# Splitting the second mixer's GELU by row tiles instead of by row chunks, with a new instruction order, in a two-layer attention and mixer kernel

## The chip, the cores and the metric

The kernel runs on one core of a Trainium2 chip. The core has a matrix engine (TensorE, PE in the profile), ScalarE (ACT), VectorE (DVE), GpSimd (POOL) and SyncE (SP), which run their own instruction streams side by side and wait for one another by semaphores. The metric is device time in microseconds (us). The kernel before has a median of 1063.17 us in three runs (1063.0 to 1063.62).

## The reference, cut to what matters

Two layers, each an attention block and a mixer block, both with a residual. S = 2048 rows, D = 448, H = 16 heads of 28, F = 1792. Layer norms have neither scale nor bias.

```python
def _A_ref(x, wqkv, wo):
    qkv = (x @ wqkv).reshape(B, S, 3, H, Dh).transpose(2, 0, 3, 1, 4)
    q, k, v = qkv[0], qkv[1], qkv[2]
    p = softmax(einsum("bhqd,bhkd->bhqk", q, k) * Dh ** -0.5)
    return einsum("bhqk,bhkd->bhqd", p, v).transpose(0, 2, 1, 3).reshape(B, S, D) @ wo

def _B_ref(x, w1, w2, w3, w4):
    h = gelu(layernorm(x) @ w1)
    # the four column quarters of h are shifted by +1, -1, +2 and -2 rows
    x1 = x + shifted(h) @ w2
    return x1 + gelu(layernorm(x1) @ w3) @ w4

x = A_x
for layer in range(2):
    x = x + _A_ref(layernorm(x), A_wqkv, A_wo)
    x = x + _B_ref(layernorm(x), B_w1, B_w2, B_w3, B_w4)
```

The change is in `gelu(layernorm(x1) @ w3) @ w4`: h2 = gelu(...) has 1792 columns for each row, held transposed in SBUF as h2T, 14 chunks of 128 of those columns ("row chunks": they lie on the partitions) by the rows of x.

## The kernel before

The 2048 rows are 16 tiles of 128. Attention goes by units of query tiles: four units of 4 in the first layer; in the second three of 4 and two of 2. For each unit, group of four heads and part of the keys, TensorE makes scores (line L1441, "QK") into PSUM, ScalarE takes their exp (L1484), and TensorE multiplies the result by V (L1511, "PV"). Exps come in 775 granules, of three PSUM banks and of two (1536 and 1024 elements a partition) in turn; indices 0 to 384 are the first layer's. The scores of granule n+2 are issued as soon as the exp of granule n has emptied its banks, so two granules are in flight. A part of the exps is made on VectorE by a polynomial instead (L1396 to L1412).

All else is woven between: layer norm and transposed rows xT (L1075; transposes by DMA, by TensorE at L1037 and L1053), the projections of K and Q (L1082; copies kT at L1091 and L1094, qT at L1087 and L1089, squares for a bound on the scores at L1101 to L1105, a correction and a bias of Q at L1134 and L1344, the maximum kmax at L1118), V (L1147, L1151), the output projection (L1587), the first mixer's GELU (L1674 for a unit, L1657 for the last), and the second mixer. Most of those matmuls are cut in four 32-column pieces that run beside each other, all by the helper at L174.

The second mixer (`t_mixB`) works on parts of 2 to 4 tiles: tiles [0,1,2], [3..6], [7..10], [11,12], [13,14,15] of the first layer, and in the second the first four of these, then 13, 14 and 15 singly, whose GELU (L1802) reads PSUM. For a part, 14 groups of matmuls with w3 (third stage) fill h2T through casts by VectorE (L1805); then the GELU runs in place over h2T in two instructions (L1817); then `w4_tile` (fourth stage) multiplies each tile by w4, 14 chunks one after the other, and adds the result to the residual x_res (L1825). The two GELU instructions each take 7 row chunks of all the part's tiles. A tile of w4 takes its PSUM bank when chunks 0 to 6 are there.

ScalarE must load a table between exp and GELU (ACT_TABLE_LOAD), 24 times in all. For the parts behind the first two units the second mixer's GELU is made to stand right behind the first mixer's (GATED).

The order on every engine is fixed when the kernel is built. Generators yield operations with a planned duration, what they read and what they write; a list scheduler (`Sched`) places them by rank, the ranks coming from the latest starts of the round before. After two rounds `reorder` shifts the ranks by a table of numbers, SEEDS (L614), and a last round gives the order of each engine. So an edit of an operation or of one number can move any instruction behind it. The planner also puts filler matmuls in places where TensorE would idle. At the start GpSimd loads rows of x by DMA (L866) and clears padding (L957 to L969); `t_setup` and `t_setup2` hold that.

## Time and profile before

| | before |
|---|---|
| median of the runs | 1063.17 us (1063.0 to 1063.62) |
| the profiled execution, its own time | 1062.37 us |
| its span (first to last instruction) | 1060.3 us |
| granted TensorE clock, mean | 0.998 |
| instructions on ScalarE / TensorE matmuls | 908 / 14218 |
| first exp starts, last exp ends | 33.48, 1014.14 us |
| DMA | 41.26 MB, mean 39 GB/s |

The span is shorter than the time of its execution by 2.07 us that lie around it. Three stretches can be told apart: 33.5 us until the first exp, 980.7 us in which exps follow one another, and 46.2 us behind the last exp, with the end of the second mixer and the output. Rows of the profile name the source line, the engine, and the tiles as out<-in; an arrow in brackets names what ended the idle time before an instruction.

### The profile page before, as it was taken

The numbers are of one execution on the slowest core, as the hardware profiler recorded it, in microseconds if no ns is written. First come the engines' busy times: TensorE is split into PE (matmuls) and PEld (weight loads), VectorE is DVE, ScalarE is ACT, GpSimd is POOL, SyncE is SP. The second block draws the span as 40 slices with busy tenths as digits, with TensorE's granted clock in tenths as the row PEclk, the third lists the DMA queues.
The fourth block names the chain that finished last, engine by engine and source line by source line (L and its number), as shares of the span: only waits on it lengthen the run. The fifth ranks groups of instructions, "written<-read, shape, count | busy, mean of one in ns | idle before, by whom it ended". The sixth has DMA issues, their size and how long they took to land.

```text
span 1060.3 us, 31768 instructions
## 1 busy us (share of the span) xinstructions
PE 986.8 (93%) x14218; PEld 390.6 (37%) x14219; DVE 840.9 (79%) x1854; ACT 1003.3 (95%) x908; POOL 161.2 (15%) x177
## 2 busy tenths in 40 slices
PE   7999999999999998999998999999999999999898
PEld 5333333333333333333334333333333333443355
DVE  8999999999968775754996689999988788545463
ACT  5899999999999999999699999999999999999954
POOL 5220101210202002100332012001112020120111
PEclk9999999999999999999999999999999999999999
DMA  7222060100000000101112222010011010010000
GB/s 203 61 74 74 25 179 22 22 16 2 22 21 22 2 21 23 21 2 42 32 51 67 75 67 72 22 42 21 11 32 37 2 34 12 22 27 25 12 19 23
DMA packets 77103, 41.26 MB, mean 39 GB/s; under 512 B 61288, under 2 KB 70376, under 8 KB 76968
## 3 DMA queue, kind: packets, MB, share of 16 engines
q1 hardware_dynamic: 74856, 35.58, 12.9%
q0 software_dynamic: 2112, 3.67, 1.4%
q8 instruction: 111, 1.82, 0.7%
q14 instruction: 24, 0.20, 0.1%
HBM read 14.20 MB, written 8.13 MB: 21 GB/s over the span
## 4 chain that ended last, share of the span: by engine, by line
ACT 73%; PE 22%; DVE 4%; issue 0%; DMA 0%; POOL 0%; DVEq 0%; ACTq 0%
ACT PT L1484 66%; PE ps L174 11%; PE ps L1441 5%; PE ps L1511 3%; ACT h2T L1817 3%; PE ps L1796 1%; ACT hT L1674 1%; PE ps L1822 1%; ACT L1484 1%; DVE xn L1075 1%; ACT L1674 1%; DVE st L984 0%; DMA w<-in_A_x_dram 0%; DVE qT L1134 0%; DVE sc L935 0%
## 5 line engine op out<-in xcount | busy, mean ns | idle before, releaser
L1484 ACT ACTIVATE PT<-ps 128x1536 bf16<-128x1536 f32 (+1 forms) x775 | 879.5, 1259 | 14.4 <-PE ps L1441 13.0
L1441 PE MATMUL ps<-qT,kT 32*128 32x512 bf16 (+1 forms) x2184 | 303.0, 359 | 30.8 <-ACT PT L1484 24.9
L1511 PE MATMUL ps<-PT,vaug 128*32 128x512 bf16 (+1 forms) x2184 | 233.0, 360 | 5.1 <-ACT PT L1484 3.5
L1441 PEld LDWEIGHTS ps<-qT,kT 32*128 32x128 bf16 x2184 | 76.0, 91 | 253.9 <-ACT PT L1484 147.0
L174 PE MATMUL ps<-xT,w 128*32 128x512 bf16 (+5 forms) x2324 | 150.6, 345 | 1.0 <-DVE h2T L1805 0.4
L1805 DVE CAST h2T<-ps 128x512 bf16<-128x512 f32 (+2 forms) x126 | 73.7, 585 | 40.5 <-PE ps L174 38.2
L1511 PEld LDWEIGHTS ps<-PT,vaug 128*32 128x32 bf16 x2184 | 61.9, 94 | 108.9 <-issue 53.8
L174 PE MATMUL ps<-w,h2T 128*32 128x448 bf16 x1524 | 94.3, 354 | 6.6 <-ACT h2T L1817 3.0
L1396 DVE TENSOR_SCALAR dT<-ps 128x512 f32<-128x512 f32 x116 | 79.1, 684 | 14.8 <-PE ps L1392 11.3
L174 PE MATMUL ps<-wk_pad,zero 128*32 128x256 bf16 x1644 | 81.0, 275 | 0.0
L1407 DVE SCALAR_TENSOR_TENSOR dU<-dF 128x512 f32<-128x512 uint16 x116 | 79.3, 684 | 0.9
L1412 DVE SCALAR_TENSOR_TENSOR dT<-dU,dT 128x512 int32<-128x512 f32 x116 | 79.4, 685 | 0.8
L1409 DVE SCALAR_TENSOR_TENSOR dU<-dF,dU 128x512 f32<-128x512 uint16 x116 | 79.1, 682 | 0.7
L174 PEld LDWEIGHTS ps<-xT,w 128*32 128x32 bf16 (+1 forms) x2324 | 53.0, 95 | 53.2 <-issue 24.6
L1825 DVE SCALAR_TENSOR_TENSOR x_res<-x_res,mst,ps 128x448 f32<-128x448 f32 x32 | 21.6, 678 | 61.2 <-PE ps L174 48.2
L1105 POOL TENSOR_TENSOR sq<-qT 128x512 bf16<-128x512 bf16 (+1 forms) x32 | 31.9, 999 | 248.9 <-DVE qT L1091 191.7
L1764 POOL TENSOR_TENSOR x_res<-x_res,x1b 128x448 f32<-128x448 f32 x31 | 37.2, 1204 | 184.7 <-DVE x1b L1745 183.2
L174 PEld LDWEIGHTS ps<-w,h2T 128*32 128x32 bf16 x1524 | 38.1, 96 | 43.4 <-issue 15.3
L1105 POOL TENSOR_TENSOR sq<-kT 128x512 bf16<-128x512 bf16 (+1 forms) x32 | 31.7, 991 | 137.3 <-DVE kT L1091 90.9
L1402 DVE TENSOR_SCALAR dF<-dT 128x512 uint16<-128x512 uint16 x116 | 48.5, 418 | 0.6
L174 PEld LDWEIGHTS ps<-wk_pad,zero 128*32 128x32 bf16 x1644 | 40.0, 95 | 23.8 <-issue 19.1
L1817 ACT ACTIVATE h2T<-h2T 128x3584 bf16<-128x3584 bf16 (+2 forms) x18 | 46.9, 2605 | 0.3
(172 smaller groups left out, 1189.3 us busy)
## 6 DMA issues: line engine op xcount, KB each, us to landing
uscr<-u_sb SPq DMA_DIRECT2D x24, 256.0 KB, 2.1
uin<-uscr SPq DMA_DIRECT2D x24, 256.0 KB, 2.8
x_res<-in_A_x_dram POOLq DMA_DIRECT2D x4, 896.0 KB, 5.3
out_dram<-uin SPq DMA_DIRECT2D x16, 112.0 KB, 1.7
w<-in_B_w_dram SPq DMA_DIRECT2D x1, 1568.0 KB, 13.4
w<-in_B_w_dram SPq DMA_DIRECT2D x1, 1344.0 KB, 8.6
h2T<-in_A_wqkv_dram SPq DMA_DIRECT2D x2, 336.0 KB, 4.5
xT<-xn SPq DMA_TRANSPOSE x33, 3.7
```

The costliest lines, as they stand in the source:

```text
L174: return [self.e.matmul(out=out[c:min(c + 32, self.m)], lhsT=lhsT[:, c:min(c + 32, self.m)], rhs=rhs, start=start, stop=stop, tile_positio ...
L1105: yield op("pool", 0.1 + 0.002 * nw, lambda e, si=si: e.tensor_tensor(out=sq[:, si, 0:nw], in0=dst, in1=dst, op=ALU.mult), reads=dkeys, wr ...
L1396: yield op("dve", c_ps(cw), lambda e, b=b: e.tensor_scalar(out=dT[:, s, 0:cw], in0=ps[:, bi(b), 0:cw], scalar1=65536.0 + 127 * 128.0, scal ...
L1402: yield op("dve", c_f2b(cw), lambda e: e.tensor_scalar(out=dF[:, f, 0:cw], in0=dT[:, s, 0:cw].bitcast(U16).rearrange("p (q two) -> p q two ...
L1407: yield op("dve", c_ps(cw), lambda e: e.scalar_tensor_tensor(out=dU[:, v, 0:cw], in0=dF[:, f, 0:cw], scalar=-16384.0, in1=dF[:, f, 0:cw], ...
L1409: yield op("dve", c_ps(cw), lambda e: e.scalar_tensor_tensor(out=dU[:, v, 0:cw], in0=dF[:, f, 0:cw], scalar=EXPD * 16384.0, in1=dU[:, v, 0 ...
L1412: yield op("dve", c_ps(cw), lambda e: e.scalar_tensor_tensor(out=dT[:, s, 0:cw].bitcast(I32), in0=dU[:, v, 0:cw], scalar=EXPC * 2.0 ** -35 ...
L1441: yield op("pe", 0.012 + W / 2400.0, lambda e, bk=bk, r0=32 * j, g=g, kc=kc, q0=q0, W=W, c0=W * h: e.matmul(out=ps[:, bk, c0:c0 + W], lhsT ...
L1484: yield op("act", e_dur(n), lambda e, b0=b0, p0=p0, cnt=cnt, cw=cw: e.activation(out=PT[:, p0:p0 + cnt, 0:cw], in_=ps[:, b0:b0 + cnt, 0:cw ...
L1511: yield op("pe", 0.004 + nt * 0.0133, lambda e, j=j, rhs=rhs, vs=vs, i=i: e.matmul(out=ps[32 * j:32 * j + 32, bi(SUM), 0:128 * nt], lhsT=v ...
L1805: yield op("dve", c_ps(NW), lambda e, fch=fch, b=b: e.tensor_copy(out=h2T[:, fch, hoff:hoff + NW], in_=ps[:, bi(b), 0:NW]), reads=[("ps", ...
L1817: yield op("act", c_act(7 * NW), lambda e, f0=f0: e.activation(out=h2T[:, f0:f0 + 7, hoff:hoff + NW], in_=h2T[:, f0:f0 + 7, hoff:hoff + NW ...
```

## The change

The GELU over h2T is split by tiles: passes over two tiles (one, where an odd one is left) and all 14 row chunks. A tile of w4 takes its bank when all 14 chunks of its tile are there. The number of passes for a part stays two for 3 and 4 tiles; for 2 tiles it becomes one. In SEEDS the entries are other ones from 29639 on (95 lines of them become 122), so instructions move on all engines, throughout. Lines of the new kernel lie 27 to 28 lower.

```diff
@@ -617,95 +617,122 @@
         (3033793134, 1, 0, -44.1), 120960, 262583, (2115317989, 1, 0, -1.4), (24560949, 2, 3, 14.3), 282526, 330535, 128665, 506082,
         (2115317989, 1, 2, -6.9), 494183, 220204, 391981, 182732, 482011, 827523, 903787, 171502, 468151, 477258, 255142, 737183, 133974,
         (873278056, 1, 0, -8.0), 659964, 702438, 411030, (2992251532, 2, 0, -20.0), 356684, 480141, 383044, (2115317989, 1, 183, -0.6),
-        211184, 29639, (446382429, 5, 0, -42.4), (2115317989, 1, 2216, -1.3), 230258, 942391, 611146, 253696, 497183, (4057997978, 1, 0,
...
+        211184, 29639, (4199727191, 6, 0, -3.4), 377439, 781968, 836653, 977732, 853990, 962485, (3017015515, 1, 0, -3.9), 788647, 843800,
...
     ]
     DL = 0.58
@@ -1812,12 +1839,13 @@
                 yield ("sig", ("h2", L, tiles[0]))
                 if gated:
                     yield ("wait", ("g2", L, tiles[0]))
-                for f0 in (0, 7):
-                    hk = [(("h2T",), (fch, hoff // 128 + j)) for fch in range(f0, f0 + 7) for j in range(n)]
-                    yield op("act", c_act(7 * NW), lambda e, f0=f0: e.activation(out=h2T[:, f0:f0 + 7, hoff:hoff + NW], in_=h2T[:, f0:f0 + 7, hoff:hoff + NW], func=ACT.Gelu_apprx_tanh),
-                             reads=allk if f0 == 0 else hk, writes=hk, tab="gelu", margin=0.0 if gated or f0 else 1.0)
+                for i in range(0, n, 2):
+                    m = min(2, n - i)
+                    hk = [(("h2T",), (fch, hoff // 128 + j)) for fch in range(14) for j in range(i, i + m)]
+                    yield op("act", c_act(14 * 128 * m), lambda e, i=i, m=m: e.activation(out=h2T[:, :, hoff + 128 * i:hoff + 128 * (i + m)], in_=h2T[:, :, hoff + 128 * i:hoff + 128 * (i + m)], func=ACT.Gelu_apprx_tanh),
+                             reads=allk if i == 0 else hk, writes=hk, tab="gelu", margin=0.0 if gated or i else 1.0)
             def w4_tile(i, t):
-                b = yield ("acq", MISC, [(("h2T",), (fch, hoff // 128 + i)) for fch in range(7)])
+                b = yield ("acq", MISC, [(("h2T",), (fch, hoff // 128 + i)) for fch in range(14)])
                 for fch in range(14):
                     yield op("pe", c_mm(D), lambda e, fch=fch, i=i, b=b: e.matmul(out=ps[:, bi(b), 0:D], lhsT=h2T[:, fch, hoff + 128 * i:hoff + 128 * i + 128], rhs=w4[:, fch, :],
                                                                            start=(fch == 0), stop=(fch == 13)),
```

Three places where the order moved. First TensorE at the boundary of the layers, from the last granule of layer 0 (one L1441 matmul, L1468 in the new kernel) to layer 1's first (five of them). The rows between are the projections of layer 1's first unit (xT with wq_pad, wk_pad, wv; sq with astat sums the squares for the bound) and the fourth stage (w,h2T; 32x448 is one column piece). Before:

```order
L1441 MATMUL ps<-qT,kT 128x512
L174 MATMUL ps<-xT,wq_pad 32x512 x28
L174 MATMUL ps<-wv,xT 32x448 x16
L174 MATMUL ps<-xT,wq_pad 32x512 x32
L174 MATMUL ps<-xT,wk_pad 32x512 x16
L174 MATMUL ps<-sq,astat 32x512 x8
L174 MATMUL ps<-xT,wk_pad 32x512 x12
L174 MATMUL ps<-sq,astat 32x512 x4
L174 MATMUL ps<-xT,wk_pad 32x512 x4
L1441 MATMUL ps<-qT,kT 128x512 x5
```

Now:

```order
L1468 MATMUL ps<-qT,kT 128x512
L174 MATMUL ps<-w,h2T 32x448 x16
L174 MATMUL ps<-xT,wq_pad 32x512 x16
L174 MATMUL ps<-w,h2T 32x448 x56
L174 MATMUL ps<-xT,wk_pad 32x512 x16
L174 MATMUL ps<-xT,wq_pad 32x512 x16
L174 MATMUL ps<-sq,astat 32x512 x4
L174 MATMUL ps<-xT,wk_pad 32x512 x12
L174 MATMUL ps<-sq,astat 32x512 x4
L174 MATMUL ps<-xT,wk_pad 32x512 x4
L1468 MATMUL ps<-qT,kT 128x512 x5
```

16 and 56 pieces of the fourth stage, its last for the part [7..10], come between the two granules now, and less of Q and K; the projection of V went behind. The GELU of the part [7..10] on ScalarE stands ahead of granule 378 instead of 370.

Second the start, on GpSimd (x_res<-in_A_x_dram are the loads of rows, sc and rstd small powers, the MEMSETs padding). Before:

```order
L992 TENSOR_TENSOR rstd<-vpe,neghalf 128x2
L866 DMA x_res<-in_A_x_dram 128x4x448
L959 MEMSET vaug 128x320
L866 DMA x_res<-in_A_x_dram 128x4x448 x2
L961 MEMSET wo_pad 128x1792
L965 COPY selq<-id 32x512
L934 TENSOR_TENSOR sc<-sc,halfs 128x4
L866 DMA x_res<-in_A_x_dram 128x4x448
L967 MEMSET w 128x448
L969 MEMSET w 128x1792
```

Now:

```order
L1019 TENSOR_TENSOR rstd<-vpe,neghalf 128x2
L893 DMA x_res<-in_A_x_dram 128x4x448 x2
L986 MEMSET vaug 128x320
L893 DMA x_res<-in_A_x_dram 128x4x448 x2
L988 MEMSET wo_pad 128x1792
L961 TENSOR_TENSOR sc<-sc,halfs 128x4
L1019 TENSOR_TENSOR rstd<-vpe,neghalf 128x4
L992 COPY selq<-id 32x512
L994 MEMSET w 128x448
L996 MEMSET w 128x1792
```

The four loads stand together more closely, ahead of the clearing of wo_pad; one rstd moved ahead of selq and the last two MEMSETs. On VectorE in the same stretch, from the first copies of xT. Before:

```order
L1057 COPY xT<-ps 128x4x128 x2
L962 MEMSET zero 128x64
L963 CAST e28b<-e 128x4
L964 TENSOR_TENSOR id<-ident 32x16
L925 CAST csum<-ps 128x8
L984 BN_STATS st<-x_res 128x6
L928 COPY wsum<-ps 128x8
L1057 COPY xT<-ps 64x4x128
L930 TENSOR_SCALAR sc<-wsum 128x4
L931 RECIPROCAL sc<-sc 128x4
L932 SCALAR_TENSOR_TENSOR sc<-wsum,sc 128x4
L986 BN_AGGR mv<-st 128x2
```

Now:

```order
L1084 COPY xT<-ps 128x4x128 x3
L1084 COPY xT<-ps 64x4x128
L1011 BN_STATS st<-x_res 128x6
L989 MEMSET zero 128x64
L1013 BN_AGGR mv<-st 128x2
L1011 BN_STATS st<-x_res 128x6
L952 CAST csum<-ps 128x8
L1013 BN_AGGR mv<-st 128x2
L1128 TENSOR_TENSOR sq<-kT 128x512
L955 COPY wsum<-ps 128x8
L1011 BN_STATS st<-x_res 128x6
L1145 TENSOR_REDUCE kmaxc<-ps 128x1
```

One copy of xT more is VectorE's (ScalarE had it), and a square of K and the first kmax come ahead of the small column sums (wsum, sc), which came ahead of all K before.

Third ScalarE behind the last exp (PT are exps, uin copies for the output, hT the first mixer's GELU, h2T the second's). Before:

```order
L1484 ACTIVATE PT<-ps 128x1024 x2
L1866 ACTIVATE uin<-x_res 128x448 x3
L1657 ACT_TABLE_LOAD
L1657 ACTIVATE hT<-ps 112x128 x8
L1817 ACTIVATE h2T<-h2T 128x7x256 x2
L1042 ACTIVATE xT<-ps 128x512
L1866 ACTIVATE uin<-x_res 128x448
L1802 ACTIVATE h2T<-ps 128x128 x42
```

Now:

```order
L1511 ACTIVATE PT<-ps 128x1024 x2
L1894 ACTIVATE uin<-x_res 128x448 x2
L1069 ACTIVATE xT<-ps 128x512
L1684 ACT_TABLE_LOAD
L1684 ACTIVATE hT<-ps 112x128 x4
L1845 ACTIVATE h2T<-h2T 128x14x256
L1684 ACTIVATE hT<-ps 112x128 x4
L1069 ACTIVATE xT<-ps 128x512
L1829 ACTIVATE h2T<-ps 128x128 x42
```

One GELU pass of 14 chunks and two tiles stands between the two halves of the first mixer's GELU, where two passes of 7 chunks stood behind both; two copies for the output went to VectorE, and a copy of xT came to ScalarE.

203 rows, old and new, of the table SEEDS are left out of this document.

## The prediction

> **What bounds the kernel now.** I read the page first: the busy shares, the chain of work that ended last, and the costliest groups (line, engine, operation, count; then busy us and mean ns of one; then the idle time before them and its releaser).
>
> ```profile
> PE 986.8 (93%) x14218; PEld 390.6 (37%) x14219; DVE 840.9 (79%) x1854; ACT 1003.3 (95%) x908; POOL 161.2 (15%) x177
> ...
> ACT 73%; PE 22%; DVE 4%; issue 0%; DMA 0%; POOL 0%; DVEq 0%; ACTq 0%
> ...
> L1484 ACT ACTIVATE PT<-ps 128x1536 bf16<-128x1536 f32 (+1 forms) x775 | 879.5, 1259 | 14.4 <-PE ps L1441 13.0
> ...
> L174 PE MATMUL ps<-w,h2T 128*32 128x448 bf16 x1524 | 94.3, 354 | 6.6 <-ACT h2T L1817 3.0
> ```
>
> ScalarE is busy 95% of the span, and 879.5 us of that are the 775 exps. An exp waited only 14.4 us in all. So a microsecond counts only where ScalarE does more work, where it waits, or where it has not begun (before the first exp) or has finished (after the last). TensorE at 93% is the close second. Its 3.0 us of waits for the GELU at L1817 lie where ScalarE is itself busy with that GELU, so taking them away pays only if a later exp was waiting for the matmuls behind them.
>
> Next, ScalarE's order of time, merged (start, duration, count), and its GELU groups by shape:
>
> ```profile
> 200.04 113.19 ACT L1484 ACTIVATE PT<-ps 128x1536 bf16<-128x1536 f32 x100
> ...
> 480.16 6.41 ACT L1817 ACTIVATE h2T<-h2T 128x3584 bf16<-128x3584 bf16 x2
> 486.60 1.28 ACT L1484 ACT_TABLE_LOAD   x1
> 487.89 16.43 ACT L1484 ACTIVATE PT<-ps 128x1536 bf16<-128x1536 f32 x15
> 512.41 12.60 ACT L1484 ACTIVATE PT<-ps 128x1024 bf16<-128x1024 f32 x11 [8.10 <-PE ps L1441]
> 526.48 15.02 ACT L1484 ACTIVATE PT<-ps 128x1536 bf16<-128x1536 f32 x13 [1.46 <-PE ps L1441]
> ...
> 545.61 1.02 ACT L1484 ACTIVATE PT<-ps 128x1024 bf16<-128x1024 f32 x1 [0.79 <-PE ps L1441]
> ```
>
> ```profile
> L1817 ACT ACTIVATE h2T<-h2T 128x3584 bf16<-128x3584 bf16 x8 | 25.5, 3184 | 0.1
> L1817 ACT ACTIVATE h2T<-h2T 128x2688 bf16<-128x2688 bf16 x6 | 14.6, 2438 | 0.1
> ...
> L1817 ACT ACTIVATE h2T<-h2T 128x1792 bf16<-128x1792 bf16 x4 | 6.8, 1694 | 0.1
> ```
>
> In the middle of a layer 100 exps follow one another in 113.19 us, 1.13 us each, with no wait. The one large hole is at the layer boundary: 8.10 us before the first exp of layer 1. It is over half of all waiting.
>
> **The change part by part.** Two things are edited, the split of the GELU and the table behind the order. The sum has six terms.
>
> *1. GELU instructions.* A part of three or four tiles has two passes before and after. Four tiles are two of 3584 elements in both. Three tiles were 2 x 2438 = 4876 ns and become one of 3584 and one of 1792, 3184 + 1694 = 4878 ns. A part of two tiles was 2 x 1694 = 3388 ns and becomes one of 3184, 0.2 less. There are two such parts: **-0.4**. Table loads stay at 24 and the exps at 775. That the first two tiles' fourth-stage matmuls are whole after the first pass, and no longer stop at chunk 7, touches the 3.0 us above. I cost it at nothing: while the GELU runs, ScalarE is the engine that is late, and its next exps have scores lying ready in both bank groups. Were the cover gone, it would cost or win at most a share of those 3.0.
>
> *2. The boundary.* The rows of TensorE and VectorE there:
>
> ```profile
> 484.18 5.12 PE L174 MATMUL ps<-w,h2T 128*32 128x448 bf16 x100 [0.20 <-DVE kmaxc L1118]
> ...
> 503.06 0.38 PE L1441 MATMUL ps<-qT,kT 32*128 32x512 bf16 x1
> ...
> 511.99 0.59 PE L1441 MATMUL ps<-qT,kT 32*128 32x512 bf16 x5
> ```
>
> ```profile
> 502.97 0.68 DVE L1825 SCALAR_TENSOR_TENSOR x_res<-x_res,mst,ps 128x448 f32<-128x448 f32 x1 [3.25 <-PE ps L174]
> ...
> 509.19 0.75 DVE L1091 TENSOR_SCALAR kT<-ps,cols 128x512 bf16<-128x512 f32 x1 [0.17 <-PE ps L174]
> 509.86 1.43 DVE L1134 SCALAR_TENSOR_TENSOR qT<-ps,sc,qT 128x512 bf16<-128x512 f32 x2
> 511.20 0.64 DVE L1344 TENSOR_SCALAR qT<-qT,bcol 128x512 bf16<-128x512 bf16 x1
> ```
>
> Layer 1's first scores start at 511.99 because layer 1's Q and K need xT, which needs x_res, which needs the last fourth-stage matmuls. All of that hangs on the end of the first GELU pass, T0 = 480.16 + 3.2 = 483.36. Before, 15 exps stand behind this GELU: ScalarE runs out at 504.32 = T0 + 21.0 and starts again at 512.41 = T0 + 29.1. In the new order only 7 exps are left when the GELU ends. ScalarE then runs out at T0 + 3.2 (second pass) + 1.3 (load) + 7 exps at some 1.06 to 1.13 (7.4 to 7.9), near T0 + 11.9, 9.05 earlier. How much earlier can TensorE have the scores? The 224 narrow w4 matmuls take 51 ns each by the row of 100, and a little less where others interleave: 10.5 us. I go through the new order: the last score of layer 0 at T0 + 10.6, 16 w4 at 11.45, 16 of Q at 12.3, two residual additions of 0.68 each that release the next bank at 12.85, 56 w4 at 15.5, 16 of K at 16.35, the last tile's addition behind normalising work on VectorE at 17.1, 16 of Q at 18.0, then the chain kT 0.75, correction of Q 0.75 and bias 0.33 with their hand-offs, 20.1, and scores and the exp at T0 + 20.9. The stall is 20.9 - 11.9 = 9.0 against 8.10: **+0.9**. From below: by TensorE's own work alone (224 w4, 32 of Q, 28 of K, 7 exps' scores) the scores start near T0 + 18.7, a stall of 6.8, -1.3. From above: one more hand-off as the 3.25 us before the addition in the row at 502.97, +3. I take the walk, as its waits all have rows here.
>
> *3. Behind the boundary* the output projection's matmuls stood 16 and 48 ahead of two scores, and the exp waited 1.46. Now they are 20, 28 and 16 ahead of three. At some 0.05 us each, 20 fewer in the largest lump take away 1.0 to 1.2 of that: **-1.1** (bounds -1.46 and 0). Farther on, 48 of w1 stand in one lump where 32 stood, ahead of the score for which the exp waited 0.79: 16 x 0.05 = 0.8, less what two banks of scores cover: **+0.5** (0 to +0.8).
>
> *4. Startup.* The first exp needs both the scores at 33.04 and, before that, a VectorE which hardly pauses:
>
> ```profile
> 9.61 5.27 DVE L1075 TENSOR_SCALAR xn<-w,mv,rstd 128x448 bf16<-128x448 bf16 x2 [0.41 <-POOL rstd L992]
> ```
>
> ```profile
> 9.53 0.97 POOL L866 DMA_DIRECT2D x_res<-in_A_x_dram  x1
> 10.49 1.54 POOL L959 MEMSET vaug<- 128x320 bf16 x1
> 11.61 1.51 POOL L866 DMA_DIRECT2D x_res<-in_A_x_dram  x2
> 13.08 1.66 POOL L961 MEMSET wo_pad<- 128x1792 bf16 x1
> ```
>
> ```profile
> L984 DVE BATCH_NORM_STATS2 st<-x_res 128x6 f32<-128x448 f32 x5 | 3.0, 602 | 0.0
> ...
> L935 DVE TENSOR_SCALAR sc<-sc,cols 128x4 f32<-128x4 f32 x1 | 2.7, 2694 | 0.0
> ...
> L1118 DVE TENSOR_REDUCE kmaxc<-ps 128x1 f32<-128x512 f32 x3 | 2.1, 684 | 0.1
> ...
> L1087 DVE TENSOR_SCALAR qT<-ps 128x512 bf16<-128x512 f32 x2 | 1.4, 681 | 0.0
> L1057 DVE COPY xT<-ps 128x512 bf16<-128x512 bf16 (+1 forms) x3 | 1.2, 419 | 0.3 <-PE ps L1053 0.3
> L1101 DVE TENSOR_TENSOR sq<-kT 128x512 bf16<-128x512 bf16 x2 | 0.9, 426 | 0.1
> ...
> L1151 DVE CAST vaug<-ps 128x448 bf16<-128x448 f32 x1 | 0.6, 614 | 0.0
> ```
>
> The groups are of VectorE from 14.9 to 33.0. Two instructions of about 0.45 us (xn) took 5.27 together while GpSimd ran its DMA issues and MEMSETs, and a tiny one (L935) took 2.7 while it ran others. In the new order VectorE does, ahead of the same bias of Q: one copy of xT more (0.42), one statistics pair (0.7), one kT (0.75), one kmaxc (0.68) and one square of K (0.43) more, and one qT (0.68), one cast of V (0.61) and a small one (0.2) less: +1.5. It waits longer for the first K, since its square now comes before Q on TensorE: the copy of K ends near 19.4, VectorE is through with its other work at 18.3, +1.1. The long wait at L935 goes, since GpSimd's last MEMSETs now come later, behind a copy that needs VectorE; there I take 0.75, the stretch of GpSimd's work that is left when VectorE comes to its next small instruction: 0.75 - 2.6 = -1.85. A fourth DMA issue (1.51 / 2 = 0.75) stands ahead of the second xn: +0.75. Two more hand-offs, TensorE to VectorE: +0.3. Sum **+1.8**. From below, the xn wait does not grow and the earlier K comes through: -1.6; from above, the late MEMSETs block as long as L935 was blocked (+1.9) and the hand-offs double: +5.
>
> *5. Tail.* TensorE's array time behind the last scores is the same within 0.2 us in both orders, by the same kinds of rows. In the new order one GELU pass of 3184 ns stands between the two halves of the first mixer's GELU, where two passes stood behind both:
>
> ```profile
> 1003.15 10.99 ACT L1484 ACTIVATE PT<-ps 128x1024 bf16<-128x1024 f32 x10
> ...
> 1029.83 3.42 ACT L1817 ACTIVATE h2T<-h2T 128x1792 bf16<-128x1792 bf16 x2
> ...
> 1050.98 2.82 PE L1822 MATMUL ps<-w,h2T 128*128 128x448 bf16 x14 [0.44 <-ACT h2T L1802]
> ```
>
> The second half comes some 3 us later, but its tile is wanted only behind 56 third-stage matmuls (63 ns each, 3.5 us): covered. At the end the last tile's third-stage matmuls stand 22 in a lump ahead of its fourth stage, not 10, so this waits for ScalarE once more, as in the last row: **+0.5** (-1.5 to +1.5).
>
> *Sum:* -0.4 + 0.9 - 1.1 + 0.5 + 1.8 + 0.5 = +2.2. On the profiled execution, 1062.37 (span 1060.3 and 2.07 around it), that is 1064.6. The median of the runs, 1063.17, is 0.80 above that execution, so the forecast is **1065.4**. The rest of the program holds another 775 exps in a new order of their helpers; their waits were some 3 us in all before, and I leave them at zero with +-1.5.
>
> **The rivals.** *R1, the boundary fills itself:* the addition's and the copy's waits do not end last and TensorE's own work does. The stall is 6.8 instead of 9.0: 1065.4 - 2.2 = 1063.2, no change. For it: TensorE has rows back to back from 484.18 to 503.06. Against it: the 3.25 us that VectorE waited for TensorE before the last addition, after which xT, Q and K still had to follow.
>
> *R2, GpSimd hands over after each instruction:* the second pair of xn would get in when the first DMA issue ends (10.50) and end near 11.7 instead of 14.88. That is 3.2 earlier than before and 3.95 earlier than my walk. The first projection of K then runs before TensorE's slow stretch, in 1.03 instead of 1.86:
>
> ```profile
> 17.48 1.86 PE L1082 MATMUL ps<-xT,wk_pad 128*128 128x512 bf16 x4 [0.60 <-DVE sc L930]
> ...
> 21.01 1.03 PE L1082 MATMUL ps<-xT,wk_pad 128*128 128x512 bf16 x4 [0.28 <-ACT sq L1103]
> ```
>
> 1065.4 - 3.95 - 0.8 = 1060.7, faster. Against it: the two xn ended at 13.2 and 14.88, by the seams of GpSimd at 13.1 and 14.74, and not at the first one, 10.5.
> [...]
>
> *R3, the clock:*
>
> ```profile
> 13.44:16.86 3.42, 1.98 (x35) 1.35 (x34) 3.07 (x9) 0.48 (x1) 1.90 (x2) 1.00 1.55 386
> 16.86:20.27 3.41, 2.81 (x8) 1.05 (x8) 3.29 (x11) 0.97 (x3) 2.37 (x4) 0.50 0.89 214
> ```
>
> The columns are the stretch, its length, the busy time of TensorE, its weight loads, VectorE, ScalarE and GpSimd, and the granted clock. In the second stretch the clock was 0.50, behind one in which TensorE was busy for 1.98 of 3.42 us. In the new order TensorE waits for the square of K right there. If a second stretch runs at half speed, four projections and their sums of some 2 us take twice as long: +2.1, 1067.5, slower.
> [...]
>
> *R4, the order doesn't act as it is written* can't be: instructions per engine are fixed and run in order.
>
> **How the numbers follow.** What a measurement of this kernel can tell from no change is 0.2%, 2.1 us: faster is below 1061.0, slower above 1065.3. The forecast F (1065.4, its own range 1063.4 to 1067.6) has 0.52, of which 0.29 lie above 1065.3, 0.22 within and 0.01 below. R1 has 0.17 (0.12 within, 0.05 faster, when the tail also comes out short). R2 has 0.17 (0.15 faster). R3 has 0.14 (0.13 slower). Sums: faster 0.21, within 0.37, slower 0.42. The range goes from 1060.5, which leaves out the better half of R2, to 1069.0, which takes in R3 and the upper bounds of boundary or startup, but not both together.
>
> **What would show it.** At the boundary: 7 exps between the load and one hole of 9.0 us (6.8 by R1; over 11 would be a wait I have missed). Behind it no hole above 0.5 before the output projection's scores. First exp at 35.3 by the walk, near 31 by R2, past 37 by R3; the third xn's row says which: 4 us or more by F, near 1 by R2. From the end of the last exp (1003.15 + 10.99 = 1014.14) to the end of the span 46.2 us now and 46.7 then. If the middle of the layers shows new holes of over 2 us in sum, the zero I gave them is the error.

## The result and the profile after

The changed kernel takes 1065.67 us, the median of six runs (1063.8 to 1067.73); the kernel before took 1062.95 beside it (1062.49 to 1063.62, six runs). The ratio is 1.0025 (95% interval 1.0016 to 1.0035): slower by a quarter of a per cent. The forecast was 1065.4. The six runs of the changed kernel lie much farther apart than those of before, and the profiled execution is the slowest of them, 1067.73.

The page of the changed kernel (busy shares, chain of work that ended last, costliest groups), in the lines that answer to those of before:

```profile
PE 985.9 (92%) x14192; PEld 392.5 (37%) x14192; DVE 842.1 (79%) x1855; ACT 1001.5 (94%) x905; POOL 160.7 (15%) x177
...
ACT 76%; PE 18%; DVE 5%; issue 1%; DMA 0%; ACTq 0%; DVEq 0%
...
L1511 ACT ACTIVATE PT<-ps 128x1536 bf16<-128x1536 f32 (+1 forms) x775 | 879.0, 1270 | 21.2 <-PE ps L1468 20.3
```

ScalarE has 1.8 us less to do than before (1003.3), but the exps waited 21.2 us instead of 14.4, nearly all of it for scores from TensorE. Where they waited, by ScalarE's order of time:

```profile
499.21 7.38 ACT L1511 ACTIVATE PT<-ps 128x1536 bf16<-128x1536 f32 x7
515.00 10.06 ACT L1511 ACTIVATE PT<-ps 128x1024 bf16<-128x1024 f32 x9 [8.41 <-PE ps L1468]
525.54 17.59 ACT L1511 ACTIVATE PT<-ps 128x1536 bf16<-128x1536 f32 x15 [0.48 <-PE ps L1468]
...
547.00 2.40 ACT L1511 ACTIVATE PT<-ps 128x1536 bf16<-128x1536 f32 x2 [2.58 <-PE ps L1468]
...
571.40 2.37 ACT L1511 ACTIVATE PT<-ps 128x1536 bf16<-128x1536 f32 x2 [1.05 <-PE ps L1468]
...
656.02 11.42 ACT L1511 ACTIVATE PT<-ps 128x1024 bf16<-128x1024 f32 x10 [3.10 <-PE ps L1468]
```

Seven exps behind the table load and then one hole of 8.41 us, as drawn in the prediction; behind it 0.48 where 1.46 stood. But three holes farther on are new or larger: 2.58 before exp 410, 1.05 before exp 426, and 3.10 before exp 485. The kernel before waited 0.79 before exp 411 and at most 0.39 near the other two.

The start, on VectorE and on GpSimd:

```profile
9.19 4.33 DVE L1102 TENSOR_SCALAR xn<-w,mv,rstd 128x448 bf16<-128x448 bf16 x4
```

```profile
9.54 1.73 POOL L893 DMA_DIRECT2D x_res<-in_A_x_dram  x2
11.26 1.51 POOL L986 MEMSET vaug<- 128x320 bf16 x1
12.35 1.51 POOL L893 DMA_DIRECT2D x_res<-in_A_x_dram  x2
13.81 1.65 POOL L988 MEMSET wo_pad<- 128x1792 bf16 x1
```

The last of the four xn (normalised rows) ended at 13.52, before at 14.88 (9.61 + 5.27). One by one, the third and the fourth before, and the fourth now:

```profile
9.61 3.61 DVE L1075 TENSOR_SCALAR xn<-w,mv,rstd 128x448 bf16<-128x448 bf16 x1 [0.41 <-POOL rstd L992]
13.14 1.74 DVE L1075 TENSOR_SCALAR xn<-w,mv,rstd 128x448 bf16<-128x448 bf16 x1
```

```profile
13.14 0.38 DVE L1102 TENSOR_SCALAR xn<-w,mv,rstd 128x448 bf16<-128x448 bf16 x1
```

The third was held nearly as long as before, 3.41 us. The fourth took 1.74 beside the MEMSET of wo_pad before; now the fourth DMA issue stands there, and it takes 0.38.

So VectorE was early, and still the first exp came at 33.72. The windows of the clock say why (TensorE, its weight loads, VectorE, ScalarE, GpSimd busy; then the granted clock):

```profile
12.20:15.64 3.44, 2.24 (x42) 1.87 (x43) 3.12 (x7) 0.88 (x1) 3.26 (x4) 1.00 1.56 401
15.64:22.47 6.83, 5.86 (x20) 2.27 (x18) 5.62 (x22) 1.91 (x3) 2.03 (x2) 0.51 1.26 308
...
346.70:350.10 3.40, 2.67 (x30) 0.93 (x26) 2.97 (x9) 3.40 (x4) 0.00 (x0) 1.00 0.00 0
350.10:353.60 3.50, 3.50 (x38) 1.29 (x35) 2.51 (x6) 2.82 (x3) 0.00 (x0) 0.52 0.00 0
```

TensorE ran at a clock of 0.50 for 6.83 us in the start (15.76 to 22.59; before 3.41, 16.86 to 20.27) and for another 3.41 us near 350 (350.27 to 353.68), where an exp (268) then waited 1.39 us.

### The profile page after: what moved, and what is told of

It reads as the page before. It is cut to its first block, busy times and chain, and to the rows that moved or that the text cites. A ratio compares the mean times of both kernels' runs of the same rounds, so it can differ in the third digit from the quotient of the medians.

```text
span 1065.9 us, 31716 instructions
## 1 busy us (share of the span) xinstructions
PE 985.9 (92%) x14192; PEld 392.5 (37%) x14192; DVE 842.1 (79%) x1855; ACT 1001.5 (94%) x905; POOL 160.7 (15%) x177
## 3 DMA queue, kind: packets, MB, share of 16 engines
q1 hardware_dynamic: 74856, 35.58, 13.6%
q0 software_dynamic: 2112, 3.67, 1.4%
## 4 chain that ended last, share of the span: by engine, by line
ACT 76%; PE 18%; DVE 5%; issue 1%; DMA 0%; ACTq 0%; DVEq 0%
ACT PT L1511 67%; PE ps L174 7%; ACT h2T L1845 4%; PE ps L1468 4%; PE ps L1538 3%; PE ps L1850 1%; ACT hT L1701 1%; ACT L1511 1%; PE ps L1823 1%; ACT L1701 1%; DVE xn L1102 1%; PE ps L1109 1%; ACT L1845 0%; DVE dT L1423 0%; DMA w<-in_A_x_dram 0%
## 5 line engine op out<-in xcount | busy, mean ns | idle before, releaser
L1511 ACT ACTIVATE PT<-ps 128x1536 bf16<-128x1536 f32 (+1 forms) x775 | 879.0, 1270 | 21.2 <-PE ps L1468 20.3
L1468 PE MATMUL ps<-qT,kT 32*128 32x512 bf16 (+1 forms) x2184 | 302.8, 359 | 40.0 <-ACT PT L1511 35.3
L1468 PEld LDWEIGHTS ps<-qT,kT 32*128 32x128 bf16 x2184 | 75.8, 91 | 268.5 <-ACT PT L1511 163.4
L174 PE MATMUL ps<-xT,w 128*32 128x512 bf16 (+2 forms) x2248 | 153.5, 354 | 1.6 <-DVE dT L1423 0.7
L174 PE MATMUL ps<-wk_pad,zero 128*32 128x256 bf16 x1876 | 88.2, 276 | 0.0
L174 PEld LDWEIGHTS ps<-xT,w 128*32 128x32 bf16 x2248 | 53.4, 95 | 55.8 <-issue 26.9
L174 PEld LDWEIGHTS ps<-wk_pad,zero 128*32 128x32 bf16 x1876 | 47.0, 96 | 22.9 <-issue 17.4
L1538 PE MATMUL ps<-dT,vaug 128*32 128x512 bf16 (+1 forms) x120 | 47.4, 400 | 0.1
```

Source lines behind the costliest of these rows:

```text
L174: return [self.e.matmul(out=out[c:min(c + 32, self.m)], lhsT=lhsT[:, c:min(c + 32, self.m)], rhs=rhs, start=start, stop=stop, tile_positio ...
L1468: yield op("pe", 0.012 + W / 2400.0, lambda e, bk=bk, r0=32 * j, g=g, kc=kc, q0=q0, W=W, c0=W * h: e.matmul(out=ps[:, bk, c0:c0 + W], lhsT ...
L1511: yield op("act", e_dur(n), lambda e, b0=b0, p0=p0, cnt=cnt, cw=cw: e.activation(out=PT[:, p0:p0 + cnt, 0:cw], in_=ps[:, b0:b0 + cnt, 0:cw ...
L1538: yield op("pe", 0.004 + nt * 0.0133, lambda e, j=j, rhs=rhs, vs=vs, i=i: e.matmul(out=ps[32 * j:32 * j + 32, bi(SUM), 0:128 * nt], lhsT=v ...
```

## The experiments

Each kernel was timed in five rounds beside the kernel before (medians of before between 1062.94 and 1063.24); exps are named by their index, and "holes" are ScalarE's waits before an exp. Where instructions were moved, the diff shows the order on the engine.

**1. The changed kernel again.** No edit.

> The changed kernel unaltered, for its spread. Theory T (the extra time is holes of the new order: 3.1 us ahead of exp 485, 2.6 ahead of exp 410, and stretches of half TensorE clock of which an execution has one to three at about 1 us each): median 1065 to 1066, single times between 1063.5 and 1068, each the longer the lower its mean clock, and the holes at exps 385, 410 and 485 in the profile again within 0.4 us. Rival C (the extra time is all clock): a profile with one slow stretch has no hole of over 1 us but the one at the layer boundary.

1066.41 us (1063.64 to 1068.39), ratio 1.003 (1.002 to 1.004). The median lies a little above the expected 1065 to 1066. The nine runs follow the mean granted clock: 1063.64 and 1063.77 at 0.999, 1065.73 at 0.997, 1066.32 to 1067.42 at 0.995, 1068.24 and 1068.39 at 0.994, close to 1 us for each thousandth. The profiled one had no slow stretch (stretch of half clock) before the end of the last exp, and yet it has the large holes of the first profile; so these are not the clock's, against rival C. The same windows there:

```profile
12.20:15.64 3.44, 2.20 (x42) 1.83 (x43) 3.12 (x7) 0.98 (x1) 3.30 (x4) 1.00 1.55 401
15.64:22.47 6.83, 5.62 (x31) 2.68 (x31) 6.29 (x24) 3.03 (x5) 2.03 (x2) 1.00 1.28 311
```

So the order without the clock can be set against the order before. The stretch from the first exp to the end of the last, before and then here:

```profile
33.48:1014.14 980.66, 919.67 (x13366) 345.94 (x13366) 786.86 (x1711) 965.45 (x825) 139.34 (x145) 1.00 0.14 35
```

```profile
31.28:1015.61 984.33, 916.35 (x13525) 347.45 (x13526) 789.71 (x1707) 964.44 (x824) 139.31 (x145) 1.00 0.14 35
```

| us | before | changed, first profile | changed, full clock |
|---|---|---|---|
| execution, span | 1062.37, 1060.3 | 1067.73, 1065.9 | 1063.77, 1062.0 |
| first exp starts | 33.48 | 33.72 | 31.28 |
| first exp to end of last | 980.66 | 985.86 | 984.33 |
| behind the last exp | 46.2 | 46.3 | 46.4 |
| hole at the boundary, exp 385 | 8.10 | 8.41 | 8.40 |
| out-projection, exps 394 to 396 | 1.58 | 0.48 | 0.48 |
| exps 409 to 411, with the fct ahead of them | 1.48 | 2.76 | 2.75 |
| exps 424 to 428 | 0.60 | 1.68 | 1.68 |
| exps 474 to 485 | 0.80 | 3.61 | 3.61 |
| exps 8 and 30 to 32 | 0.28 | 0.82 | 0.81 |
| exp 268 | 0 | 1.39 | 0 |

The rows add up the waits that the timeline marks, those of 0.1 us and more. Against the profile before, the new order at full clock starts 2.2 us earlier, then loses 3.67 between the first exp and the last (4.7 more waiting, 1.0 less work on ScalarE) and 0.2 behind: 1.7 in the span. The 2.2 need not all be the order's: the profile before has 3.41 us of half clock in its start, and no run of that kernel beside the experiments shows a mean clock above 0.998. The holes agree to 0.02 us from one execution to the other, except that at 268, which goes with a slow stretch. In the median, low clock adds some 2 us to the 1063.7 of full clock.

**2. The old split in the new order.** Each GELU of the second mixer again in two passes of 7 chunks; every other instruction as in the changed kernel.

```diff
-ACTIVATE h2T<-h2T 128x14x256
-ACTIVATE h2T<-h2T 128x14x128
+ACTIVATE h2T<-h2T 128x7x384 x2
...
-ACTIVATE h2T<-h2T 128x14x256 x2
+ACTIVATE h2T<-h2T 128x3584 x2
```

> The order of the changed kernel on every engine, but each pair of GELU passes cut by row chunks again (parts of two tiles in two passes). T: 0.0 to 0.8 us slower than the changed kernel (0.2 us for each of two two-tile parts, and waits of the first two tiles for the second pass): 1065.5 to 1066.5. Rival S (the split by tiles itself costs, since the fourth stage of the last tiles waits longer for a whole pass): 1 us or more faster, 1064.7 or below.

1072.54 us (1068.88 to 1074.04), ratio 1.0085 (1.0072 to 1.0097), at clocks of 0.989 to 0.995: a miss of 6 us. At the same clock of 0.995 it is 1068.88 against 1066.32 to 1067.42 for the changed kernel. All holes are there again, 8.40 at the boundary among them, and one more:

```profile
500.52 2.37 ACT L1541 ACTIVATE PT<-ps 128x1536 bf16<-128x1536 f32 x2
503.62 5.12 ACT L1541 ACTIVATE PT<-ps 128x1536 bf16<-128x1536 f32 x5 [0.74 <-PE ps L1498]
```

The tiles' w4 matmuls stop at chunk 7 and with them the scores of exp 380: 0.74. With two GELUs 0.24 longer that is some 1.2 for the split, so the new split is the better one in this order. The rest went with slow stretches: 10.2 us at a clock of 0.51 in the start (13.5 to 23.7) and 10.2 at 0.51 near 755 (754.2 to 764.4); by the profiled execution's mean clock of 0.989 some 3 us more lay elsewhere, an estimate. Why this kernel fell into more of them was not tried.

**3 and 4. Split and table exchanged.** The changed kernel with the table of before, and the kernel before with the new table (entries shortened in the diff).

```diff
 SEEDS = [
...
-        211184, 29639, (4199727191, 6, 0, -3.4), 377439, 781968,
+        211184, 29639, (446382429, 5, 0, -42.4), (2115317989, 1, 2216, -1.3),
...
```

> The GELU split by tiles with the old table of numbers. T: the split moves the planned times a little, so the order differs again and has its own holes; the time is before plus what these are, 1062.5 to 1067, and its exps wait for scores as many us more than before's 14.4 us as the time is longer, within 1.5. Rival S: as slow as the changed kernel with exps that wait no longer than before.

> The GELU split by row chunks with the new table. T: slower than before by its holes, 1063 to 1070. Rival S: as fast as before within 0.5 us, since the split is what costs.

1106.94 us (ratio 1.041, 1.0396 to 1.0423) and 1090.77 (1.0257, 1.0244 to 1.027): both expectations missed by far. The largest single hole of either stands where ScalarE waits for VectorE's dbc ahead of exp 410, of the first and then of the second:

```profile
567.85 0.21 ACT L1246 ACTIVATE fct<-dbc 128x4 f32<-128x4 f32 x1 [9.83 <-DVE dbc L1244]
```

```profile
555.99 0.21 ACT L1273 ACTIVATE fct<-dbc 128x4 f32<-128x4 f32 x1 [10.81 <-DVE dbc L1271]
```

Each of the two tables fits its own split alone. So this change can't be halved: wrongly paired, the kernels lie 41 and 24 us behind the changed one (1066.41 beside them), and the 2.7 us between before and changed are the difference of two fitted orders.

**5. Holding the clock.** 30 more operations of filler matmuls in the places ahead of slow stretches.

```diff
 MATMUL ps<-ones_bf,h2T 128x1 x5
+MATMUL ps<-wk_pad,ident 32x256 x56
 MATMUL ps<-ident,xn 128x128
...
+MATMUL ps<-wk_pad,ident 32x256 x20
 MATMUL ps<-sq,astat 128x512
...
-MATMUL ps<-qT,kT 128x512 x5
+MATMUL ps<-qT,kT 128x512 x3
+MATMUL ps<-wk_pad,ident 32x256 x20
+MATMUL ps<-qT,kT 128x512 x2
```

> The changed kernel with 30 filler matmuls more (of four pieces each) where TensorE waits: 14 before the third tile's transposes, 5 before the first sum of squares, 5 near exp 264 and 6 near exp 567. Theory T (half the extra time is the clock): mean clock 0.998 or more in nearly all runs, spread under 1.5 us, median 1063.8 to 1064.8, some 2 us under the changed kernel's 1066.4; the holes at exps 385, 410 and 485 as before. Rival O (the order's holes are all of it, and slow stretches lie where nothing waits): clock up, time the same within 0.7 us.

1065.83 us (1065.56 to 1066.33), ratio 1.0025 (1.0015 to 1.0034); clock 0.998 to 1.000 in all eight runs. The spread falls from 4.8 to 0.8 us and the hole at 268 is gone, so the spread is the clock's. The median did not come down to the expected 1063.8 to 1064.8, though: the fillers stand in the way in the start: first exp at 32.85, 1.57 later than in experiment 1 at full clock. Holding the clock this way cost what it saved.

**6. The last part of the first layer's second mixer earlier.** Its rank in the planner is lowered by 12 us, since its GELU stands before exp 466 and stood before exp 456.

```diff
+SHIFT = ((85, 32, 1, 1, 3), -12.0)
...
+            for (t, i) in plan:
+                if t[:len(SHIFT[0])] == SHIFT[0]:
+                    plan[(t, i)] += SHIFT[1]
```

> The changed kernel, with the ranks of the tasks of layer 0's last second-mixer part (tiles 13 to 15) 12 us earlier, so that its GELU stands 6 exps earlier on ScalarE; other instructions behind it move too (some 5% of TensorE's rows). T: the hole ahead of exp 485 (3.1 us) shrinks to under 1 us, and at equal clock the time falls by 2 to 3 us. Rival (that hole is set by the chain kT, kmax, bias of Q behind the last keys alone): the hole stays above 2 us.

1076.35 us (1074.82 to 1077.34), ratio 1.0122 (1.0109 to 1.0135), a miss: the GELU came 6 exps earlier, some 5% of TensorE's rows moved with it, and the hole at 485 grew:

```profile
662.47 2.37 ACT L1514 ACTIVATE PT<-ps 128x1024 bf16<-128x1024 f32 x2 [9.06 <-PE ps L1471]
```

That the GELU is late is not enough to explain this hole, as far as a run with so many moves can tell; that it stays above 2 us is what the rival said. What its scores wait for in the changed kernel shows on VectorE and on TensorE:

```profile
653.07 0.42 DVE L1145 TENSOR_REDUCE kmaxc<-ps 128x1 f32<-128x256 f32 x1
653.53 0.16 DVE L1256 TENSOR_REDUCE k<-kmaxc 128x1 f32<-128x5 f32 x1
...
655.10 0.34 DVE L1371 TENSOR_SCALAR qT<-qT,dcol 128x512 bf16<-128x512 bf16 x1
```

```profile
654.87 0.66 PE L174 MATMUL ps<-sq,astat 128*32 128x256 bf16 x8 [0.46 <-DVE dcol L1264]
655.59 0.59 PE L1468 MATMUL ps<-qT,kT 32*128 32x512 bf16 x5
```

Q must be shifted by a new bound, the bound needs the maxima of K's last tiles, and these come through the residual, xT, wk_pad, kT and the sums of squares, with pieces of V between them.

**7 and 8. Undoing the holes by hand.** First the hole at 410 alone: VectorE corrects Q before it casts hT, and scores go ahead of w1.

```diff
-CAST hT<-ps 112x512
 SCALAR_TENSOR_TENSOR qT<-ps,sc,qT 128x512
-COPY u_sb<-ps 128x512
 TENSOR_SCALAR qT<-qT,bcol 128x512
+CAST hT<-ps 112x512
+COPY u_sb<-ps 128x512
...
 MATMUL ps<-wk_pad,ident 32x256 x12
+MATMUL ps<-qT,kT 128x512 x3
 MATMUL ps<-xT,w 32x512 x3
```

> The changed kernel with the correction and bias of Q moved ahead of a cast of hT on VectorE, and the scores of one granule moved ahead of 40 pieces of w1 matmuls on TensorE; nothing else moves. T: the hole of 2.58 us ahead of exp 410 falls to 0.5 to 1.0, and the time by 1.5 to 2.0 at equal clock. Rival (the w1 work is due later and the hole comes back within 20 exps): the sum of the holes from exp 405 to 432 (4.5 us beside the table loads) stays within 0.7.

1066.6 us (1066.04 to 1068.28), ratio 1.0035 (1.0022 to 1.0048), a miss. Exp 410 no longer waits for scores, but for the PV matmuls, and longer:

```profile
543.61 1.45 ACT L1536 ACTIVATE PT<-ps 128x1536 bf16<-128x1536 f32 x1 [3.13 <-PE ps L1563]
```

Then both holes, with the eight PV matmuls taken along at 410, and at 485 the shift of Q and the scores ahead of pieces of V and kT.

```diff
+MATMUL ps<-qT,kT 128x512 x3
+MATMUL ps<-PT,vaug 32x512 x8
 MATMUL ps<-xT,w 32x512 x3
...
-MATMUL ps<-wv,xT 32x448 x16
 MATMUL ps<-xT,wk_pad 32x256 x16
-MATMUL ps<-sq,astat 32x256 x8
 MATMUL ps<-qT,kT 128x512 x5
+MATMUL ps<-wv,xT 32x448 x16
+MATMUL ps<-sq,astat 32x256 x8
```

> The changed kernel with two local changes of order. Ahead of exp 410: on VectorE the correction and bias of Q and the copy of the PV sums ahead of a cast of hT, on TensorE the scores and then the PV matmuls ahead of 40 pieces of w1. Ahead of exp 485: on VectorE the chain kmax, bias, qT ahead of a cast of V and two copies of kT, on TensorE the scores ahead of V's projection. Theory T (each of these two holes is a wait behind work that isn't yet due): the hole at 410 falls from 2.6 to under 1.5, that at 485 from 3.1 to 2.0 to 2.5, and the time at equal clock by 1 to 2 us. Rival L (the work is due soon after, so the holes come back within 20 exps): the sum of the holes from 405 to 432 and from 470 to 500 falls by under 0.7.

1069.06 us (1066.85 to 1075.83), ratio 1.0049 (1.0037 to 1.0061); the runs at full clock took 1066.85 to 1066.94, 3.2 more than the changed kernel at full clock; a miss. Each hole was cut and came back one or two granules later:

```profile
545.97 1.45 ACT L1537 ACTIVATE PT<-ps 128x1536 bf16<-128x1536 f32 x1 [1.62 <-PE ps L1564]
550.02 1.02 ACT L1537 ACTIVATE PT<-ps 128x1024 bf16<-128x1024 f32 x1 [2.60 <-PE ps L1445]
```

```profile
656.99 2.36 ACT L1537 ACTIVATE PT<-ps 128x1024 bf16<-128x1024 f32 x2 [2.43 <-PE ps L1494]
663.02 1.02 ACT L1537 ACTIVATE PT<-ps 128x1024 bf16<-128x1024 f32 x1 [3.67 <-PE ps L1494]
```

At 410 that is 1.62 + 2.60 for 2.58. The 3.67 fell into a slow stretch of this execution (656.7 to 670.3, clock 0.51) and is no measure of the order alone. In both places the work that was put back came due almost at once, as the rival had it: neither exchange paid.

**9 to 12. The start.** The kernel before, first: the fourth load of rows follows the others, and the MEMSETs of wo_pad and w go out of the start, behind exps 60 to 76 of the plan.

```diff
 MEMSET vaug 128x320
-DMA x_res<-in_A_x_dram 128x4x448 x2
-MEMSET wo_pad 128x1792
+DMA x_res<-in_A_x_dram 128x4x448 x3
...
-DMA x_res<-in_A_x_dram 128x4x448
-MEMSET w 128x448
-MEMSET w 128x1792
...
+MEMSET wo_pad 128x1792
+MEMSET w 128x448
 TENSOR_TENSOR sq<-qT 128x512 x3
+MEMSET w 128x1792
```

> The kernel before, with the fourth load of rows ahead of the MEMSET of wo_pad on GpSimd, and the MEMSETs of wo_pad and of the two weight paddings behind exps 60, 68 and 76; nothing else moves. T (MEMSETs hold up VectorE's xn and L935, DMA issues do not): the fourth xn ends at 13.5 instead of 14.9, L935 takes 0.2 instead of 2.7, the first exp starts at 30.5 to 32, the time falls by 1.5 to 3 us. Rival (TensorE's slow stretch and the column sums set the start): under 0.7 us less.

1062.2 us (1061.12 to 1069.7), ratio 0.9997 (0.9986 to 1.0009): the first exp starts at 29.84, 3.6 earlier, in a start without a slow stretch (the first projections of K and of Q, four matmuls each, took 1.02 and 1.03; before, 1.86 and 1.59 in the slow stretch). The time misses the expected 1.5 to 3 us: the start's gain is given back, in part beside the MEMSETs' new places (they ran at 87.84, 89.37 and 117.70), as at this exp behind the MEMSET of w at 117.70:

```profile
121.77 9.16 ACT L1509 ACTIVATE PT<-ps 128x1536 bf16<-128x1536 f32 x8 [0.80 <-PE ps L1466]
```

Of the other two holes there, 0.82 and 0.98 at exps 53 and 54, the second lay in a slow stretch (91.7 to 95.1, clock 0.53), so MEMSETs and clock are not told apart in it. One MEMSET, of vaug, still stood between the loads, and held the third xn for 2.88 us. So next all MEMSETs but one go into the 4.7 us in which GpSimd waits early on, and the loads follow one another.

```diff
 AFFINE_SELECT e<-ones_f 128x4 x2
-TENSOR_TENSOR rstd<-vpe,neghalf 128x2
-MEMSET xn 128x8x64
+MEMSET wo_pad 128x1792
+MEMSET w 128x448
 MEMSET vaug 128x320x4
 TENSOR_TENSOR rstd<-vpe,neghalf 128x2
-DMA x_res<-in_A_x_dram 128x4x448
+MEMSET xn 128x8x64
 MEMSET vaug 128x320
-DMA x_res<-in_A_x_dram 128x4x448 x2
-MEMSET wo_pad 128x1792
+TENSOR_TENSOR rstd<-vpe,neghalf 128x2
+DMA x_res<-in_A_x_dram 128x4x448 x4
```

> The kernel before with GpSimd's MEMSETs of wo_pad, one weight padding and two of V's padding ahead of its first powers, where GpSimd waited 4.7 us for VectorE, all four loads of rows one after the other, and the last MEMSET behind the power that follows them; nothing else moves. T (the MEMSETs in the start cost before some 3 us through VectorE's xn and L935): first exp at 29.5 to 30.5 as in the run with the MEMSETs put off, no new holes between exps 50 and 80, median 1059 to 1060.5. Rival (DMA issues hold xn as well, or the last MEMSET holds another instruction): first exp 31 to 33, median 1061 or more.

1061.35 us (1059.68 to 1062.47), ratio 0.9985 (0.9977 to 0.9994), faster than before by a little, but short of the expectation. First exp at 30.91 at full clock, the holes as before. The rows of VectorE and of GpSimd:

```profile
9.89 0.96 DVE L1100 TENSOR_SCALAR xn<-w,mv,rstd 128x448 bf16<-128x448 bf16 x2 [0.41 <-POOL rstd L1017]
...
22.77 1.42 DVE L1100 TENSOR_SCALAR xn<-x_res,mv,rstd 128x448 bf16<-128x448 f32 x1
```

```profile
9.80 3.21 POOL L891 DMA_DIRECT2D x_res<-in_A_x_dram  x4
...
22.36 1.58 POOL L994 MEMSET w<- 128x1792 bf16 x1
```

Two xn took 0.96 us together while four DMA issues ran, against 5.27 for the same pair before. The one xn that met the remaining MEMSET took 1.42 (0.51 otherwise), which is the second half of the rival. So an xn beside a MEMSET is held, and DMA issues alone hold it by 0.27 us at most (the fourth xn took 0.65 here and 0.38 in the changed kernel). A mixture is not explained by that: the third xn took 3.61, 3.41 and 2.88 in the kernels with a MEMSET between the issues (before, changed, experiment 9), and it was already held 0.9 to 1.5 us ahead of the MEMSET's own row and past its end. Without the MEMSET it takes 0.40; which instruction holds it outside that row is open.

Last, that MEMSET and the load of w3 behind it go out of the start too, in the kernel before and in the changed one.

```diff
-MEMSET w 128x1792
...
 TENSOR_TENSOR mst<-mst,neghalf 128x4
+MEMSET w 128x1792
 TENSOR_TENSOR x_res<-x_res,x1b 128x448
```

> The kernel before, its instructions the same, with the padding MEMSETs of GpSimd off the way of VectorE's first normalised rows (wo_pad, one w pad and both vaug into GpSimd's early wait, the loads of rows one after another) and, other than in the run before, the last MEMSET of w with the load of w3 behind it put off to the GELU behind exp 142. Theory (a MEMSET of GpSimd holds VectorE's xn, a DMA issue does not): no xn longer than 0.7 us, the first exp at 29.8 to 30.2 at full clock (33.48 before, 30.91 with the last MEMSET still in the startup), the holes behind it as before (8.1 at exp 385, 1.46 at 396), 1058.6 us at full clock, median near 1060.3. Rival: the last MEMSET costs in the middle what it cost at the start, a hole of 0.8 us or more near exp 142, and the median is that of the run with the MEMSET in the startup, 1061.3.

> The changed kernel, its instructions the same, with the same edit of the startup: wo_pad and both vaug MEMSETs and one w pad in GpSimd's early wait, the last MEMSET and the load of w3 behind exp 149. Theory (the startup and the rest add up; MEMSETs hold xn): the third and fourth xn are done by 11.5 us (13.5 in the changed kernel), the first exp starts at 29.5 to 30 at full clock (31.28), the other holes stay within 0.05 us (8.40 at exp 385, 2.58 at 410, 3.10 at 485), and the time is 1 to 1.5 us under the changed kernel's at equal clock, some 1062.4 at full clock, median 1063.5 to 1065.5; so it stays 2 us or more above the kernel before with the same edit, and that difference lies between exps 386 and 490. Rival: the low-clock windows of TensorE fall elsewhere, and the median is the changed kernel's, 1065.7 to 1066.4.

The kernel before with this start: **1060.53 us** (1059.13 to 1061.63), ratio 0.9977 (0.9968 to 0.9986), the fastest of this study, 2.4 us under before and 5 under the changed kernel. Full clock gave 1059.13 and 1059.73 where 1058.6 was expected. The MEMSET ran at 173.46, near exp 124, and no hole came there, though it held xn as well: four took 3.15 us, 1.77 before.

```profile
172.55 3.15 DVE L1659 TENSOR_SCALAR xn<-x_res,mv,mst 128x448 bf16<-128x448 f32 x4
```

```profile
173.46 1.58 POOL L994 MEMSET w<- 128x1792 bf16 x1
```

Where no exp was waiting for that xn, the same instruction cost nothing. The first exp came at 31.22, in an execution with one slow stretch in its start (3.40 us at a clock of 0.54, 16.20 to 19.60), as the kernel before has it in its profile (33.48): 2.26 earlier at like clock. The expected 29.8 to 30.2 at full clock was not seen.

The changed kernel with this start: 1064.28 us (1062.89 to 1066.88), ratio 1.0012 (1.0003 to 1.0021). The four xn end at 10.83:

```profile
9.42 1.41 DVE L1127 TENSOR_SCALAR xn<-w,mv,rstd 128x448 bf16<-128x448 bf16 x4
```

The holes are unchanged (8.40, 2.58, 3.10). At full clock it takes 1062.89 to 1063.06, only 0.6 to 0.9 under the changed kernel: 1 to 1.5 was too much. The rest of the start waits for other things, in this profile among them an x_res load (1.63 us); its first exp came at 33.13, with 6.80 us at a clock of 0.52 in the start (15.40 to 22.20). Against the kernel before with the same start it stays 3.75 us behind, in the medians and in the fastest runs (1062.89 - 1059.13 = 3.76). The table above has 3.67 between the first exp and the last for the two orders: so the difference lies there, and not in the start.

## Why the prediction came out as it did

The number held to 0.3 us, and the sign. The way to it was right in half of its steps, and that errors of both signs cancelled was luck: at full clock the first exp came 2.2 us earlier where +1.8 was forecast, the middle lost 4.4 in places that had been left at zero, and low clock put the median 1.9 above the full-clock execution, where the sum had 0.80 between a profiled execution and the median.

- **GELU instructions, -0.4: right.** The GELU before exp 431 takes 5.81 us with its loads, before 6.05; there are two such parts. The stop of w4 at chunk 7, costed at nothing, is worth 0.74 in the new order (experiment 2).
- **The boundary, +0.9: right in form, size +0.3.** Seven exps and one hole, 8.41 instead of 9.0. The end that TensorE's work alone would give (R1, 6.8) did not come.
- **Behind the boundary, -1.1: right,** 1.58 became 0.48. **The lump of w1, +0.5: mis-sized,** +1.3 over exps 409 to 411. It is not the lump of 16 matmuls alone: with the scores in front of it, the exp waited for PV (experiments 7 and 8).
- **The start, +1.8: the failed step is "a fourth DMA issue stands ahead of the second xn: +0.75".** The fourth xn ran beside that issue in 0.38; the MEMSET of wo_pad, which stood there before, had held it for 1.74. So the last xn came 1.36 earlier and not 0.75 later. Two more terms were off at full clock: the small instruction at L935 (L962 now) took 0.21 instead of 2.69, a gain of 2.5 for 1.85, and VectorE's longer wait for the first K, +1.1, was 0.38. At full clock the first exp came 2.2 earlier. How much of that is the slow stretch in the profile before is not known; in the changed kernel 6.83 us of half clock cost 2.4 (33.72 against 31.28), so an estimate for 3.41 us is 1.2. R2 was right that the start would gain, and wrong in how: the third xn took 3.41, neither the 4 or more of the forecast nor near 1. And R3 happened as well, shown by the clock in three of the six profiled executions that keep this start: the first profile (0.50 for 6.83 us), experiment 2 (0.51 for 10.2) and experiment 6 (0.8 in the first fortieth of its span, as in the first profile). The first exp came at 33.28 to 35.06 in these and in experiment 8, and at 31.28 and 31.12 in 1 and 7: with its 6.83 us of half clock the first profile was back at +0.24.
- **The tail, +0.5: +0.1 to +0.2.** Within its bounds.
- **"The rest of the program ... zero with +-1.5" is the error that the prediction named for itself.** Exps 474 to 485 lost 2.8, 424 to 428 lost 1.1, exps 8 to 32 lost 0.5: 4.4 us of new holes at full clock, of which ScalarE's own work (-1.0) and smaller waits gave some back. In the profiled execution 1.4 at exp 268 came on top, by the clock.

So the change did not cost 2.7 us where the prediction put them. At full clock the boundary and its neighbours lose little (+0.3 - 1.1 + 1.3), the start is a gain, and most of the loss lies farther on, at exps 424 to 485. By the rows of experiment 6, the hole at 485 is where the last part of the mixer has to be through before the next K is whole. That the holes there belong to this order is shown (they repeat to 0.02 us, and stay with either split and either start). Which choice of the planner makes them is open: an earlier GELU made the one at 485 worse, and local exchanges moved those at 410 and 485 on.

What starts a slow stretch was not shown. TensorE was busy for 2.67 of 3.40 us ahead of the one at 350; and in the start 2.24 of 3.44 us were followed by half clock in the first profile, 2.20 of 3.44 by full clock in experiment 1.

## What to carry to other kernels

Before a small change of the order is judged, repeat the kernel and sort its runs by granted clock: here equal instructions lay 4.8 us apart, more than the change was worth. A fitted order belongs to the code that it was fitted to; exchange half of the pair and the time tells of the misfit alone. Look in the startup for MEMSETs of GpSimd beside VectorE's first xn and move them into GpSimd's own waits; that gave 2.4 us, nearly as much as the change cost.

## What the hardware showed unexpectedly

- A MEMSET on GpSimd held VectorE's xn: a pair that takes 0.96 us beside DMA issues alone took 5.27, and a single one of 0.51 took 1.42. Four DMA issues on GpSimd, 3.21 us long, held the two xn beside them by 0.27 us at most. Where one xn met one MEMSET, it ended just behind it: before at 14.88 (13.14 + 1.74), the MEMSET of wo_pad at 14.74; in experiment 10 at 24.19 (22.77 + 1.42), the MEMSET of w at 23.94. The third xn before (9.61, for 3.61 us) spans more than one instruction of GpSimd: the MEMSET of vaug and the DMA issues ahead of it and behind it.
- The clock was halved in the start and in the middle of the kernel, in stretches of 3.41 us (clock 0.50, before and first profile), 6.83 (0.50, first profile), 10.2 (0.51, experiment 2) and 13.6 (0.51, experiment 8). Just ahead of such a stretch TensorE was busy for 1.32 of 3.40 us in experiment 11 (12.80 to 16.20) and for 2.67 of 3.40 in the first profile (346.70 to 350.10, nearly all matmuls of 32 rows or 32 columns). Between two executions of the same kernel the same window was granted 0.51 and 1.00.
